# Moving four epilogue steps between two groups of a fused gated-attention and SoLU kernel: copies out of PSUM removed, finish(0), finish(1) and the next load of alpha moved ahead in the order

## The chip, the cores and the metric

The kernel runs on one core of a Trainium2 chip. The metric is the device time of one execution in microseconds (us), as the median of the runs; the profile shows one such execution. The engines of a core run side by side and wait for one another by semaphores: TensorE (PE; PEld is its loading of weights), VectorE (DVE), ScalarE (ACT), GpSimd (POOL) and SyncE (SP), which issues DMAs.

## The reference

Inputs q, k, v, alpha have the shape (4, 8, 768, 48): batch B, heads H, tokens S, head size D. For each batch and head a state is carried over the tokens:

```
state = alpha[t, :, None] * state + outer(k[t], v[t])
y[t]  = q[t] @ state
```

The y of all heads are laid side by side, 384 values per token (DM), and the 3072 tokens go through one block:

```
h    = x @ w_in                       # 384 -> 1024 (DFF)
solu = h * softmax(h)
ln   = (solu - mean) / sqrt(var + 1e-6) * g_ln
out  = ln @ w_out                     # 1024 -> 384
```

All arrays are float32 in the kernel; the weights come as float64 and are converted on the chip.

## The kernel before, in words

**Groups and chunks.** The tokens are cut into G = 6 groups of 128 positions; a group holds those positions of all 4 batches, so 512 tokens, or four *chunks* of 128 tokens each. Chunk n belongs to group n // 4 and batch n % 4. Attention is done chunk-wise for a group (scores within the 128 positions, plus a carried state); the block is done group by group.

**The steps of attention for a group g.** alpha_T(g) transposes alpha on VectorE into aT (L205); alpha_over(g) (L210) reads the loaded alpha twice on ScalarE for a check of its range; only after it may load(alpha, an, g + 1) (L138) fill the same buffer. scan_back(g, i) (L224) makes products of alpha from the end into hT, scan_on(g, i) (L229) products from the start into aT; both run on VectorE in three parts, and scan_on(g, 2) also has ScalarE copy fend. keys and queries are multiplied by these products into kT, qv and qe; apart() (L245) splits qe on ScalarE. scores(g, half) (L275) writes four PSUM banks a0 to a3 from PE; masked(half) (L289) moves them on VectorE under the triangular mask into sT, and scores of the other half need these banks again. decay(g) (L256) scales the carried state on GpSimd. read_state (L330) and read_values (L343) make y in the banks a0 to a3 on PE; read_values ends with four copies of y by ScalarE into x (L351). next_state(g) (L353) updates the state.

**The steps of the block.** up_mm(g, f) (L385) is h = x @ w_in for one of eight slices f of DFF, into one of two PSUM buffers "h"; up_act (L395) makes e = exp(h) on ScalarE, u = h * e on VectorE and u squared on ScalarE. down(n, half) (L494) multiplies u of chunk n by w_out, four *steps* (values of f) per half, into a PSUM tile "o", of which there are two buffers (ps_o, L73): o of chunk 2 needs the buffer of chunk 0 to be free, o of chunk 3 that of chunk 1. w_out has one column of ones more (DM + 1), so that the sum of u comes with the product. finish(n) (L511) reads that sum on VectorE (L523 to L528), for group 0 adds mean_sb times the sum (L533), takes the power -1/2 on GpSimd (L537, r), scales on ScalarE (L539, o_sb) and stores through SP (L540). mean(half) (L625) makes mean_sb out of w_out on PE, with ScalarE copying each half out of an "h" buffer. in_range(i) (L579) checks a piece of the float64 weights with two reads by ScalarE; bits(i) (L589) converts it on VectorE; scaled(i) (L613) multiplies by the gain on ScalarE.

**What sets the order.** The program is written under a manual schedule: every engine runs its instructions in the order of the program text, and each waits at the head of its queue until what it needs is there. The change lies in a stretch written out by hand, L757 to L827, between the loop over the slices of group 0 (L726) and the planned loop for groups 1 to 5 (L894). It ends group 0 (its down and finish), does attention for group 1, and prepares chunk 2 of attention ("group 2": alpha, scans, keys). The first PE work behind it is up_mm(1, 0) (L908).

In the kernel before, moved(n) (L505) copies o of chunk n, with its sum, from PSUM to SBUF on ScalarE as soon as down(n) is complete; finish(n) then works on the copy, so o of chunks 2 and 3 can begin while finish(0) and finish(1) are still to come:

```
down(2, 0); down(2, 1); scores(1, 0); masked(0)
finish(0); finish(1); alpha_over(1); load(alpha, an, 2)
down(3, 0); scores(1, 1); masked(1); finish(2); alpha_T(2)
```

Seven of the eight steps of down(3) come before read_values(1) on PE: down(3, 0) and three steps of down(3, 1), two and one of them between the parts of read_state. The last step of down(3, 1) and finish(3) come behind read_values(1).

Of the kernel before, what the change touches and what calls it, by code (L numbers as in the profile page):

```python
# [9 lines left out]
FP = mybir.dt.float32  # L10
# [6 lines left out]
P = 128  # L17
# [15 lines left out]
def fast_path(ctx, tc, q, k, v, alpha, moe_w_in, moe_w_out, moe_g_ln, out):  # L33
# [12 lines left out]
    nc = tc.nc  # L46
    B, H, S, D = q.shape
    NTOK, DM = out.shape
# [8 lines left out]
    HF = FC // 2  # L57
# [4 lines left out]
    def pool(name, bufs, **kw):  # L62
        return ctx.enter_context(tc.tile_pool(name=name, bufs=bufs, **kw))
# [4 lines left out]
    work = pool("work", 2)  # L68
# [65 lines left out]
    st = [dict() for _ in range(N)]  # L134
# [3 lines left out]
    def load(src, dst, g):  # L138
        t = slice(g * P, (g + 1) * P)
        for b in range(B):  # L140
            nc.sync.dma_start(
                out=dst[32 * b : 32 * b + 32].rearrange("t h u d -> t h (u d)"),
                in_=src[b, :, t, :].rearrange("h (t u) d -> t h (u d)", u=TQ),
            )
# [100 lines left out]
    def apart():  # L245
        for i in range(2):
            nc.scalar.mul(
                out=qv[:, H : 2 * H].rearrange("p (j i) t -> p j i t", i=2)[:, :, i], in_=qe, mul=parity[:, i : i + 1]
            )
# [6 lines left out]
    def decay(g):  # L256

        if g == 0:
            return
        for i in range(2):  # L260
            for rows, d in ((0, h4[:, i:H:2, 1:2]), (H, h4[:, H:NB, 1:2])):
                s = state[:, rows + i : rows + H : 2, all_of[i]]
                nc.gpsimd.tensor_tensor(out=s, in0=s, in1=d.to_broadcast([P, NP, D]), op=ALU.mult)  # L263
            nc.gpsimd.tensor_scalar(
                out=ends_state[:, :, i], in0=state[:, H + i : 2 * H : 2, last_of[i]], scalar1=parity[:, i : i + 1],
                scalar2=None, op0=ALU.mult,
            )

    def quarter(b):
        return slice(32 * b, 32 * b + 32)  # L270
# [18 lines left out]
    def masked(half, batches=range(B)):  # L289
        a = masks[half]  # L290
        for b in batches:
            nc.vector.tensor_tensor(  # L292
                out=sT[:, b, half * NP : half * NP + NP], in0=a[b], in1=mask[:, None, :].to_broadcast([P, NP, P]),
                op=ALU.mult,
            )

    def keys_back(g, t=None):
        t = t or banks("tp", [NP, P], 3)
        for j in range(NB):
            nc.tensor.transpose(out=t[j // NP][:, j % NP], in_=kT[:, j], identity=ident)  # L300
        for i in range(3):
            nc.scalar.copy(out=kg[:, NP * i : NP * i + NP], in_=t[i])
# [18 lines left out]
    def read_begin():  # L321
        reading["y"] = {}
        reading["begun"] = set()
# [54 lines left out]
    def u_of(g, f):  # L378
        return slots[((0, 5, 4), (1, 2, 3))[g % 2][f // 3]][:, T4 * (f % 3) : T4 * (f % 3) + T4]
# [114 lines left out]
    def down(n, half, part=slice(0, HF)):  # L494
        g, b = divmod(n, B)
        d = st[n]
        if half == 0 and part.start == 0:
            d["o"] = ps_o.tile([P, 512], FP, tag="o", name="o")
        for f in range(half * HF + part.start, half * HF + part.stop):
            nc.tensor.matmul(  # L500
                d["o"][:, 0 : DM + 1], lhsT=u_of(g, f)[:, b * P : b * P + P], rhs=w_out[:, f], start=(f == 0),
                stop=(f == FC - 1), skip_group_check=True,
            )

    def moved(n):  # L505

        o = work.tile([P, DM + 1], FP, name="o_mean")
        nc.scalar.copy(out=o, in_=st[n]["o"][:, 0 : DM + 1])
        st[n].update(o=o, moved=True)

    def finish(n):  # L511
        g, b = divmod(n, B)
        d = st[n]
        s, o = sums[:, n], d["o"][:, 0:DM]
        t0 = b * S + g * P
        if g == G - 1:
            o_sb = work.tile([P, DM], FP, name="o_sb")
            r = gr[g]["r"][:, b : b + 1]
            nc.scalar.activation(out=o_sb, in_=o, func=AF.Copy, scale=r)
            nc.scalar.dma_start(out=out[t0 : t0 + P, :], in_=o_sb)  # L520
            d.clear()
            return
        nc.vector.tensor_copy(out=s[:, 0:1], in_=d["o"][:, DM : DM + 1])  # L523
        t = small.tile([P, 1], FP, name="t")
        nc.vector.scalar_tensor_tensor(
            out=t, in0=s[:, 0:1], scalar=-1.0 / DFF, in1=s[:, 0:1], op0=ALU.mult, op1=ALU.mult
        )
        nc.vector.tensor_tensor(out=s[:, 3:4], in0=t, in1=gr[g]["s"][:, b : b + 1], op=ALU.add)  # L528
        if g == 0:

            if not d.get("moved"):
                o = work.tile([P, DM + 1], FP, name="o_mean")[:, 0:DM]
            nc.vector.scalar_tensor_tensor(  # L533
                out=o, in0=mean_sb, scalar=s[:, 0:1], in1=d["o"][:, 0:DM], op0=ALU.mult, op1=ALU.add
            )
        r = small.tile([P, 1], FP, name="r")
        nc.gpsimd.tensor_tensor(out=r, in0=s[:, 3:4], in1=mhalf, op=ALU.pow)  # L537
        o_sb = work.tile([P, DM], FP, name="o_sb")
        nc.scalar.activation(out=o_sb, in_=o, func=AF.Copy, scale=r)  # L539
        nc.sync.dma_start(out=out[t0 : t0 + P, :], in_=o_sb)  # L540
        d.clear()
# [35 lines left out]
    made = {}  # L577

    def in_range(i):  # L579


        if not float64:
            return
        hi = raws[i][:, :, :, 1].bitcast(FP)
        sq = one.tile([P, F], FP, name="sq").rearrange("p (c f) -> p c f", c=hi.shape[1])
        nc.scalar.activation(out=sq, in_=hi, func=AF.Square, accum_out=far[:, i, 0:1])  # L586
        nc.scalar.activation(out=sq, in_=sq, func=AF.Exp, scale=-(2.0**24), accum_out=far[:, i, 1:2])
# [37 lines left out]
    def mean(half):  # L625


        m = ps_h.tile([P, 512], FP, tag="h", name="sums")[:, 0:DM]
        if half == 0:
            for f in range(FC):  # L630
                r = quarter(f % 4)
                nc.tensor.matmul(
                    m[r], lhsT=ones[:, 0:32], rhs=w_out[:, f, 0:DM], start=f < 4, stop=f >= FC - 4,
                    tile_position=(0, r.start), skip_group_check=True,
                )
            made["m"] = work.tile([P, DM + 1], FP, name="o_mean")[:, 0:DM]
            nc.scalar.mul(out=made["m"], in_=m, mul=-1.0 / (32 * DFF))
        else:
            nc.tensor.matmul(m, lhsT=ones, rhs=made["m"], start=True, stop=True)
            nc.scalar.copy(out=mean_sb, in_=m)  # L640
# [32 lines left out]
    def three(name, where):  # L673
        return [pool.tile([P, NP, P], FP, tag=tag, name=f"{name}{i}") for i, (pool, tag) in enumerate(where)]
# [14 lines left out]
    for i in range(3):  # L689
        part = slice(NP * i, NP * i + NP)  # L690
# [6 lines left out]
    for i in (2, 0, 1):  # L697
        if i == 1:
            scan_on(0, i)
        part = slice(NP * i, NP * i + NP)  # L700
        nc.vector.tensor_tensor(  # L701
            out=qe if i == 2 else qv[:, part], in0=t[i], in1=aT[:, part, 1:SW], op=ALU.mult
# [68 lines left out]
    for i in range(3):  # L771
        scan_back(1, i)
        part = slice(NP * i, NP * i + NP)
        nc.vector.tensor_tensor(out=kT[:, part], in0=tk[i], in1=hk[:, part], op=ALU.mult)

    down(0, 1, slice(0, 2))
    mean(0)
    down(0, 1, slice(2, HF))
    moved(0)
    mean(1)  # L780
    in_range(5)
    down(1, 1)
    moved(1)
    tq += three("tp_q2", [(ps_h, "h")])
    turned(qn, ends_q, tq, range(H, NB))
    load(q, qn, 2)
    in_range(6)
    keys_back(1, three("tp", [(ps_a, "a2"), (ps_a, "a3"), (ps_h, "h")]))
    scan_on(1, 2)
    nc.vector.tensor_tensor(out=qe, in0=tq[2], in1=aT[:, H:NB, 1:SW], op=ALU.mult)  # L790
    apart()
    decay(1)
    in_range(7)
    for i in range(2):
        scan_on(1, i)
        part = slice(NP * i, NP * i + NP)
        nc.vector.tensor_tensor(out=qv[:, part], in0=tq[i], in1=aT[:, part, 1:SW], op=ALU.mult)
    down(2, 0)
    down(2, 1)
    scores(1, 0)  # L800
    masked(0)
    finish(0)
    finish(1)
    alpha_over(1)
    load(alpha, an, 2)
    down(3, 0)
    scores(1, 1)
    masked(1)
    finish(2)
    alpha_T(2)  # L810
    read_begin()
    for batches, part in (((0, 1), slice(0, 2)), ((2, 3), slice(2, 3))):
        down(3, 1, part)
        for n in range(len(parts)):
            read_state(n, batches)
    alpha_over(2)
# [6 lines left out]
    scan_on(2, 2)  # L823
    scan_on(2, 0)
    read_values(1)
    down(3, 1, slice(3, HF))
    finish(3)  # L827


# [64 lines left out]
    for g in range(1, G + 1):  # L894
# [10 lines left out]
        for s in range(FC):  # L905
# [17 lines left out]
            if step:  # L923
                n, half = step
# [23 lines left out]
    def compare(out, x, bound, op):  # L948
# [6 lines left out]
        out=chunks[:, :, 2], in0=sums[:, :, 2], scalar=0.25, in1=sums[:, :, 3], op0=ALU.mult, op1=ALU.is_le  # L955
# [6 lines left out]
    else:  # L962
# [9 lines left out]
        out=bad, in0=all_ok[0:1, 0:1], scalar1=float(P * ends[-1]), scalar2=None, op0=ALU.is_lt  # L972
# [451 lines left out]
```

## Time and profile before

| what | value |
|---|---|
| median of 3 runs | 391.65 us (391.28 to 392.57) |
| profiled execution, its own time | 391.28 us |
| its span, first to last instruction | 389.5 us |
| mean granted TensorE clock | 0.985 |
| busy in the span | PE 369.6 (95%), DVE 244.3 (63%), ACT 148.3 (38%), POOL 127.5 (33%) |
| alpha_over(1) on ACT, start | 94.00 us |
| alpha for chunk 2: first issue by SP, transposed from | 97.38 us, 103.97 us |
| read_values(1) on PE | 99.63 to 105.66 us |
| up_mm(1, 0) on PE, start | 112.10 us |

The page gives busy time by engine, a strip of the span in 40 slices (a digit is the busy share in tenths; PEclk is the clock granted to TensorE, in tenths), the chain of work that ended last, and groups of instructions by line. The other views are the trace's own: the waits (which engine waited for which, how long), the chain in order of time, the timeline (instructions of a window in order of time), and windows (busy time of each engine, clock and DMA share in a stretch). Instructions are named by tile and line: "PE o L500" is a matmul into o at line 500, which is down.

### The profile page before, as it was taken

What the parts mean: (1) busy time and instruction counts of PE and PEld (TensorE: products, weight loads), DVE (VectorE), ACT (ScalarE), POOL (GpSimd) and SP (SyncE); (2) the same over time, 40 slices, a digit from 0 to 9 for tenths busy, and PEclk for the clock granted to TensorE, in tenths of its full rate; (3) what the DMA queues carried; (4) which work ended last, traced back from release to release, by engine and by line L of the source; (5) the groups of instructions that cost most, each with busy time, mean ns of one, the idle gap of its engine ahead of it and who ended that gap; (6) DMA issues with size and microseconds to landing.
All of it is one profiled execution on the core that took longest, in us unless ns stands there. A gap on an engine that the chain in (4) does not pass through costs nothing.

```text
span 389.5 us, 10523 instructions
## 1 busy us (share of the span) xinstructions
PE 369.6 (95%) x4659; PEld 222.4 (57%) x4659; DVE 244.3 (63%) x379; ACT 148.3 (38%) x265; POOL 127.5 (33%) x132
## 2 busy tenths in 40 slices
PE   8869999999749999999999999999999999999995
PEld 8766345566525457556656656566555575555552
DVE  0985878987398877594655793665894511444410
ACT  3637775474324516125252224153223231333111
POOL 5030000042041994246423346422544620333210
PEclk9989999999969999999999999999999999999999
DMA  9981999301467300674000863000600000000011
GB/s 186 257 221 55 235 264 183 83 0 44 104 143 122 82 3 4 94 173 101 22 2 24 129 141 97 22 4 22 97 6 22 22 24 2 21 20 20 22 43 48
DMA packets 65510, 30.78 MB, mean 79 GB/s; under 512 B 47016, under 2 KB 63664, under 8 KB 65456
## 3 DMA queue, kind: packets, MB, share of 16 engines
q1 hardware_dynamic: 64432, 29.10, 34.5%
q10 hardware_dynamic: 1024, 0.92, 0.7%
q8 instruction: 38, 0.62, 0.7%
q14 instruction: 16, 0.13, 0.1%
HBM read 25.30 MB, written 4.72 MB: 77 GB/s over the span
## 4 chain that ended last, share of the span: by engine, by line
PE 67%; DVE 14%; ACT 7%; DMA 4%; SPq 4%; issue 3%; POOL 0%; ACTq 0%
PE o L500 28%; PE h L389 23%; PE y L315 9%; PE a L281 4%; DMA room<-in_v_dram 3%; SPq L153 2%; DVE room L404 2%; DVE aT L222 2%; DVE hT L222 2%; DMA an<-in_alpha_dram 1%; ACT sq L586 1%; DVE sT L292 1%; DVE aT L197 1%; PE kv L364 1%; PE tp L300 1%
## 5 line engine op out<-in xcount | busy, mean ns | idle before, releaser
L389 PE MATMUL h<-x,w_in 128*128 128x512 f32 x288 | 133.9, 604 | 6.1 <-ACT x L351 5.6
L500 PE MATMUL o<-w_out,room 128*128 128x385 f32 x384 | 133.8, 491 | 0.0
L500 PEld LDWEIGHTS o<-w_out,room 128*128 128x128 f32 x384 | 71.2, 190 | 55.8 <-issue 13.9
L389 PEld LDWEIGHTS h<-x,w_in 128*128 128x128 f32 x288 | 53.5, 192 | 66.0 <-issue 49.3
L404 DVE TENSOR_TENSOR room<-h,e 128x512 f32<-128x512 f32 x40 | 27.6, 690 | 82.4 <-ACT e L403 82.3
L403 ACT ACTIVATE e<-h 128x512 f32<-128x512 f32 x40 | 23.9, 597 | 107.7 <-PE h L389 107.7
L420 POOL TENSOR_TENSOR p<-p,e 128x512 f32<-128x512 f32 x30 | 41.8, 1395 | 16.0 <-ACT e L403 15.9
L537 POOL TENSOR_TENSOR r<-sums,mhalf 128x1 f32<-128x1 f32 x20 | 14.9, 745 | 79.6 <-DVE sums L528 79.5
L405 ACT ACTIVATE u<-room 128x512 f32<-128x512 f32 x40 | 25.2, 630 | 35.8 <-DVE room L404 35.8
L292 DVE TENSOR_TENSOR sT<-a,mask 128x512 f32<-128x512 f32 x42 | 26.1, 681 | 8.0 <-PE a L281 7.9
L243 POOL TENSOR_TENSOR kT<-kT,hT 128x1024 f32<-128x1024 f32 (+1 forms) x8 | 14.2, 1792 | 49.6 <-DVE kT L197 49.6
L315 PE MATMUL y<-sT,vn 128*32 128x128 f32 x768 | 25.1, 286 | 5.4 <-DVE sT L292 2.9
L263 POOL TENSOR_TENSOR state<-state,hT 128x192 f32<-128x192 f32 x20 | 11.2, 580 | 55.1 <-DVE hT L222 55.1
L222 DVE TENSOR_TENSOR_SCAN hT<-aT,unit 128x516 f32<-128x516 f32 x18 | 23.1, 1336 | 8.0 <-ACT aT L683 7.9
L222 DVE TENSOR_TENSOR_SCAN aT<-aT,seed 128x516 f32<-128x516 f32 x18 | 27.3, 1547 | 0.2
L420 DVE TENSOR_TENSOR p<-p,u 128x512 f32<-128x512 f32 x30 | 23.0, 768 | 6.5 <-ACT u L405 6.5
L315 PEld LDWEIGHTS y<-sT,vn 128*32 128x32 f32 x768 | 22.4, 115 | 7.7 <-issue 4.1
L281 PEld LDWEIGHTS a<-qv,kT 32*128 32x128 f32 x704 | 21.9, 186 | 8.0 <-issue 2.4
L281 PE MATMUL a<-qv,kT 32*128 32x128 f32 x704 | 24.7, 278 | 1.2 <-DVE qv L701 0.5
L214 ACT ACTIVATE sq<-an,mone 128x1536 uint8<-128x1536 f32 x12 | 18.9, 1573 | 6.4 <-DMA an<-in_alpha_dram 6.2
L315 PE MATMUL y<-qv,state 32*32 32x128 f32 x960 | 16.8, 277 | 0.0
L539 ACT ACTIVATE o_sb<-o,r 128x384 f32<-128x384 f32 x16 | 9.3, 581 | 18.7 <-POOL r L537 18.7
(146 smaller groups left out, 372.2 us busy)
## 6 DMA issues: line engine op xcount, KB each, us to landing
an<-in_alpha_dram SPq DMA_DIRECT2D x20, 192.0 KB, 4.2
vn<-in_v_dram SPq DMA_DIRECT2D x10, 384.0 KB, 5.2
out_dram<-o_sb SPq DMA_DIRECT2D x20, 192.0 KB, 1.9
room<-in_moe_w_in_dram SPq DMA_DIRECT2D x6, 512.0 KB, 6.5
room<-in_moe_w_out_dram SPq DMA_DIRECT2D x8, 384.0 KB, 3.9
kn<-in_k_dram SPq DMA_DIRECT2D x16, 192.0 KB, 4.3
qn<-in_q_dram SPq DMA_DIRECT2D x16, 192.0 KB, 3.6
kn<-in_k_dram SPq DMA_DIRECT2D x4, 384.0 KB, 5.7
```

The source lines that it names most:

```text
L214: nc.scalar.activation(out=sq, in_=x, func=AF.Relu, scale=sign, bias=mone, accum_out=over[:, g, i : i + 1])
L222: nc.vector.tensor_tensor_scan(out=o, data0=a, data1=s, initial=1.0, op0=ALU.mult, op1=ALU.add)
L281: nc.tensor.matmul(a[b][:, i], lhsT=kT[quarter(b), kb], rhs=qv[quarter(b), qb], start=kb == h, stop=kb != h, tile_position=(32 * b, 0), sk ...
L292: nc.vector.tensor_tensor(out=sT[:, b, half * NP : half * NP + NP], in0=a[b], in1=mask[:, None, :].to_broadcast([P, NP, P]), op=ALU.mult,)
L315: nc.tensor.matmul(y_bank(b)[quarter(r), a], lhsT=lhsT, rhs=rhs, start=(b, r) not in begun, stop=stop, tile_position=(row, 32 * r), skip_g ...
L389: nc.tensor.matmul(h, lhsT=w_in[:, a, f * P : (f + 1) * P], rhs=d["x"][:, a].rearrange("p b t -> p (b t)"), start=(a == 0), stop=(a == KC ...
L403: nc.scalar.activation(out=e, in_=h, func=AF.Exp)
L404: nc.vector.tensor_tensor(out=u, in0=h, in1=e, op=ALU.mult)
L405: nc.scalar.activation(out=u2, in_=u, func=AF.Square)
L420: eng.tensor_tensor(out=p, in0=d[0][i] if f == 1 else p, in1=d[f][i], op=ALU.add)
L500: nc.tensor.matmul(d["o"][:, 0 : DM + 1], lhsT=u_of(g, f)[:, b * P : b * P + P], rhs=w_out[:, f], start=(f == 0), stop=(f == FC - 1), skip ...
L537: nc.gpsimd.tensor_tensor(out=r, in0=s[:, 3:4], in1=mhalf, op=ALU.pow)
```

## The change

The function moved() and its two calls go; finish(n) of group 0 reads o in PSUM and writes a new tile. The tile o_mean loses its extra column. In the stretch by hand, mean(0) comes ahead of all of down(0, 1); in_range(6) comes ahead of down(1, 1); finish(0) comes behind apart() and ahead of decay(1); down(2, 1) comes behind scores(1, 0); finish(1), alpha_over(1) and load(alpha, an, 2) come ahead of masked(0); down(3, 0) is done in two halves between the parts of read_state, and all of down(3, 1) comes behind read_values(1). Nothing is added; the number of matmuls stays the same.

```
-    def moved(n):
-        o = work.tile([P, DM + 1], FP, name="o_mean")
-        nc.scalar.copy(out=o, in_=st[n]["o"][:, 0 : DM + 1])
-        st[n].update(o=o, moved=True)
...
-            if not d.get("moved"):
-                o = work.tile([P, DM + 1], FP, name="o_mean")[:, 0:DM]
+            o = work.tile([P, DM], FP, name="o_mean")
...
-    down(0, 1, slice(0, 2))
     mean(0)
-    down(0, 1, slice(2, HF))
-    moved(0)
+    down(0, 1)
     mean(1)
     in_range(5)
+    in_range(6)
     down(1, 1)
-    moved(1)
     tq += three("tp_q2", [(ps_h, "h")])
     turned(qn, ends_q, tq, range(H, NB))
     load(q, qn, 2)
-    in_range(6)
     keys_back(1, three("tp", [(ps_a, "a2"), (ps_a, "a3"), (ps_h, "h")]))
     scan_on(1, 2)
     nc.vector.tensor_tensor(out=qe, in0=tq[2], in1=aT[:, H:NB, 1:SW], op=ALU.mult)
     apart()
+    finish(0)
     decay(1)
     in_range(7)
...
     down(2, 0)
-    down(2, 1)
     scores(1, 0)
-    masked(0)
-    finish(0)
     finish(1)
     alpha_over(1)
     load(alpha, an, 2)
-    down(3, 0)
+    masked(0)
+    down(2, 1)
     scores(1, 1)
     masked(1)
     finish(2)
     alpha_T(2)
     read_begin()
-    for batches, part in (((0, 1), slice(0, 2)), ((2, 3), slice(2, 3))):
-        down(3, 1, part)
+    for batches, part in (((0, 1), slice(0, HF // 2)), ((2, 3), slice(HF // 2, HF))):
+        down(3, 0, part)
         for n in range(len(parts)):
             read_state(n, batches)
...
     read_values(1)
-    down(3, 1, slice(3, HF))
+    down(3, 1)
     finish(3)
```

## The prediction

> **What bounds the kernel now.** The page first. TensorE (PE) is busy 95% of the span, so time can only come from its few holes. The busy line shows one real hole, in slices 10 and 11 counted from 0 (97 to 117 us), and in the second of them the granted clock is low too:
>
> ```profile
> PE   8869999999749999999999999999999999999995
> ...
> PEclk9989999999969999999999999999999999999999
> ```
>
> Second the waits: what ended PE's idle time from 60 to 125 us. Columns: total us, times, longest.
>
> ```profile
> PE h L389 <- ACT x L351: 5.6, 1, 5.6
> PE y L315 <- issue: 2.0, 1, 2.0
> PE tp L300 <- DVE kT L774: 0.6, 1, 0.6
> ```
>
> The 5.6 us are up(1,0), the first projection of group 1, waiting for ScalarE's copies of y. Third, the chain that ended last, in order of time (start, us, what), says why those copies are late:
>
> ```profile
> 81.38 5.19 PE o L500 x16
> 86.57 1.99 PE a L281 x55
> ...
> 88.59 2.48 DVE sT L292 x4
> ...
> 92.58 0.87 POOL r L537
> ...
> 94.00 1.66 ACT sq L214 x2
> ...
> 98.76 5.19 DMA an<-in_alpha_dram
> ...
> 103.97 2.12 DVE aT L197
> ...
> 118.16 0.56 POOL r L537
> ...
> 118.74 0.61 ACT o_sb L539
> ...
> 119.36 0.49 ACT e L403
> ```
>
> Read it upwards: e(1,0), the first exponential, stands in ScalarE's queue behind finish(3), that in VectorE's queue behind the scans of chunk 2, those behind the load of alpha for chunk 2, that behind alpha_over(1) on ScalarE, that behind finish(1), that behind masked(0), and masked(0) behind scores(1,0) and eight down steps on PE. The copies of y stand behind the same scans, through the fend copy of scan_on(2,2). So this stretch is set by the moment at which alpha_over(1) starts: 94.00 us.
>
> **The change, part by part.** I go by the timeline's starts; PE, VectorE (DVE), ScalarE (ACT), GpSimd (POOL).
>
> 1. *moved(0), moved(1) go.* Two ACT copies of 0.48 us (74.92, 78.16), and in_range(6), which stood behind the second, starts at once behind in_range(5). I cost this at nothing: ACT's next copies (kg, 80.45) wait for transposes of kT, and DVE's chain reaches the last kT at 80.67 either way. Without that cover it would be a gain of at most 0.96.
>
> 2. *mean(0) ahead of down(0,1).* PE is free at 70.40, but mean(0) needs the PSUM bank that DVE's transpose of cols frees at 71.40; it ran 71.89 to 73.32 and will run about 71.5 to 72.9. PE stands 1.1 us, and the work to the end of keys_back moves from 81.38 to about 81.6. Nothing again, since PE then waits anyway (3).
>
> 3. *finish(0) ahead of decay(1) and two scans.* DVE: its four instructions took 90.99 to 91.97, so 0.98; they now start after qe (82.89) and end near 83.85, and the last product qv ends at 87.60 instead of 86.62. PE: down(2,0) takes the PSUM buffer that moved(0) used to free at 75.4; now it waits for finish(0), 81.6 to 83.85, a new idle of 2.2. It ends at 86.45 (2.6 for four steps: sixteen instructions took 5.19), and scores(1,0) waits until 87.60 for the bank that the last qv reads: 1.1 more, and 1.03 later than before (86.57). POOL: r(0) at about 83.4 to 84.3 (0.9, as at 91.61) stands ahead of decay(1), whose six instructions took 4.75 without their waits; it ends at 88.95, not 84.28. PE's read_state, which needs it, comes at 96. ACT: in_range(7) stands behind o_sb(0) and ends at about 86.9, before anyone needs ACT. SP: one more store stands ahead of alpha's load, issued (0.4) near 85, when SP's queue is empty (nothing from 73.1 to 93.1 in the profile).
>
> 4. *finish(1), alpha_over(1) and alpha's load ahead of masked(0).* This is the gain. finish(1) no longer waits for scores and masks: DVE 87.60 to 88.58. Its r(1) on POOL stands behind decay(1): 88.95 + 0.55 (the two later r's) = 89.5; o_sb(1) 89.6; alpha_over(1) at 90.1, against 94.00: **3.9 earlier**. Bounds: with POOL free r(1) would start at 88.1 and alpha_over at 89.3 (4.7 earlier); with decay(1) at its whole 6.18 (78.10 to 84.28, waits counted) and r at 0.9 it starts near 91.9 (2.1 earlier). The load then goes out at 93.5 instead of 97.38, and alpha lands at 100.1 instead of 103.97. DVE is free for it: masked(1) and finish(2) end near 98.0 (5). Four loads and one store move earlier with their order kept.
>
> 5. *What is late next: PE's own chain.* From 87.60 with measured lengths: scores(1,0) 2.05, down(2,1) 2.79, scores(1,1) 1.99 (masked(0), 89.6 to 92.05, is ready in time) end at 94.4; masked(1) 94.5 to 97.0. Two steps of down(3,0) 1.5, read_state 1.78, two more steps 1.4 (73.32 to 74.72), read_state 2.05: 101.2 (before: 99.62, although three steps fewer stand ahead of it). read_values took 5.97 with its 2.04 us stall, 3.93 without: it ends at 107.2 or 105.2. Then all four steps of down(3,1), 2.75, where one stood before: they fill what was idle. up(1,0) starts at 109.95 or, without the stall, when the copies are done: scans end at 110.28 - 3.9 = 106.4, the copies (110.43 to 112.05) at 108.2. It started at 112.10, and slowly: 4.38 against 2.79 at full clock.
>
> 6. *Where both meet.* up(1,2) started at 120.62, on DVE's release of h. DVE and ACT bring that to 120.62 - 3.9 = 116.75. PE, with the stall, gets there at 109.95 + 2.79 + 1.47 (kv) + 2.73 = 116.95. The later one decides: 3.7 earlier. From there PE is busy to the end in an unchanged order (134 to 389 us: 250 of 255), so the shift is kept.
>
> Sum: the profiled execution took 391.28 (389.5 in the span, 1.8 around it), so 387.6. The median of the runs, 391.65, lies 0.37 above it; the forecast for a median is **387.9**.
>
> **Two costs that the trace bounds only loosely.** The stall: PE stops for 2.04 us inside read_values for nothing the profile shows, while the load of alpha fills the DMA engines:
>
> ```profile
> 100.00:102.00 2.00, 1.58 (x59) 1.31 (x48) 0.00 (x0) 0.00 (x0) 0.00 (x0) 1.00 1.04 220
> 102.00:104.00 2.00, 0.38 (x16) 0.39 (x20) 0.03 (x1) 0.00 (x0) 0.00 (x0) 1.00 0.25 77
> ```
>
> (Columns: window, length, busy us and instructions of PE, PEld, DVE, ACT, POOL, then clock, DMA share, GB/s.) The page's instruction queue moved 38 packets for 0.62 MB; PE's 9318 instructions over 38 are some 245 to a packet. From 92.4 to 107 us PE will issue some 424 short matmuls with their loads, 848 instructions, so 3 to 4 packets, some of them under a load of alpha (93.5 to 100.1, and the next from about 103.5). Between no stall and four, I take one of 2.04 as seen.
> The Trainium skill ("Runtime: NRT & Kernel Launch", Instruction fetch mechanics) holds that instructions come in blocks of 256 and that crossing one is mostly hidden; by it the stall would cost nothing and the shift would be the 3.9 of part 4.
>
> The clock: idle of 2.86 us (22.25 to 25.10) is followed by 0.62 and 0.52 of the full clock from 26 to 30, and 120 matmuls of y then took 5.15, against 3.74 at the rate of the 128 later ones (3.99): 1.4 lost. The 2.04 us stall left the clock at 1.00. My new idles, 2.2 and 1.1 with 2.6 us of matmuls between, lie nearer the stall: I take no loss, with 1.4 to 1.6 (4.38 - 2.79) as the other end.
> The Trainium skill ("TensorE: Matmul & The Clock Gate", Part 1: The HAM clock gate) has the clock fall after an idle window of about 3.4 us; by it neither idle would cost anything, though the 2.86 us row shows that less was enough here.
>
> **The rivals.** (a) *The clock falls* at 83.9 us, or decay(1) is as slow as its bound: PE's chain loses 1.6, or alpha's chain keeps 2.1 of 3.9; the shift is about 2.1: 389.5. For it: the 2.86 us row. Against: a stall of 2.04 did nothing.
> (b) *A second stall.* Each adds 2.04 to PE's chain, which has 0.0 to spare: 3.7 - 2.04 = 1.6, so 390.0.
> (c) *Slower:* PE's chain becomes the bound and stalls three times more in read_state, read_values and kv, because both loads of alpha now lie beside dense matmuls, where the second lay beside an idle PE: 3.7 - 6.1 = 2.4 slower, 394.1. It decides once the added stalls exceed 3.7 us. For it: 3 to 4 packets fall in that stretch; against: one stall in the whole profile before.
> (d) *Nothing moves:* the gain of 3.7 is given back by two more stalls, or alpha's load takes its time under PE's fetches: within 1.2 us of 391.65.
>
> **Numbers.** Forecast 0.58, (a) 0.13, (b) 0.11, (d) 0.09, (c) 0.09. Faster by over 0.3% (1.2 us, about what a measurement of this kernel can tell from no change): 0.58 + 0.13 + 0.11 = 0.82; within it 0.09; slower 0.09. The range leaves out (c) and (d), 0.18: from the early bound of part 4 (391.65 - 4.7, so 386.9) to (b) with a little more, 390.4.
>
> **What would show it.** Right: alpha_over(1) starts near 90.1, alpha lands near 100.1, PE waits for finish(0) near 82 to 84 and hardly for x before up(1,0), which runs at full clock from about 110. Wrong: POOL's r(1) later than 91; the clock below 1.0 between 84 and 92; more than one wait of PE for "issue"; or up(1,2) near 120 although alpha landed at 100, in which case a later bound hid the shift.

## The result, and the profile after

| | before | after |
|---|---|---|
| median | 391.46 us (4 runs, 391.11 to 392.57) | 385.86 us (4 runs, 384.77 to 386.53) |
| profiled execution, its span | 391.28, 389.5 | 386.53, 384.7 |
| TensorE busy in the span | 369.6 | 367.6 |
| mean granted clock | 0.985 | 0.995 |

The ratio is 0.9849, 95% interval [0.9816, 0.9883]: 5.6 us less by the medians. The forecast was 387.9 in a range from 386.9 to 390.4, so the sign held and the size was too small by 2 us; the time lies below the range.

The strip of the page has no hole any more in slices 10 and 11, and the clock is full there; a smaller one has come in slices 7 and 8, where PE now waits for mean(0)'s bank and for finish(0):

```profile
PE   8769999879999999999999999999999999999995
...
PEclk9989999999999999999999999999999999999999
```

The waits of PE in after, 60 to 125 us (total us, times, longest). The 5.6 us for x are gone, and the stall for "issue" has shrunk from 2.0 to 0.2. Four waits are new, and all are for VectorE: o_mean is finish(0), cols is the bank of mean(0), room is the release of h for up(1,2), and qv is the bank of scores(1,0):

```profile
PE o L500 <- DVE o_mean L526: 2.4, 1, 2.4
PE sums L625 <- DVE cols L460: 1.0, 1, 1.0
PE h L389 <- DVE room L404: 0.8, 1, 0.8
PE a L281 <- DVE qv L787: 0.4, 1, 0.4
PE y L315 <- issue: 0.2, 1, 0.2
```

The chain of after in order of time (start, us, what). masked(0) is no longer a link between the scores and alpha's load; from the load on, the same steps follow as before, some 4 to 5 us earlier:

```profile
88.10 2.06 PE a L281 x62
90.16 2.79 PE o L500 x8
92.95 0.56 PE a L281 x13
93.53 0.34 SPq L141
...
94.91 4.36 DMA an<-in_alpha_dram
99.29 2.21 DVE aT L197
...
113.78 0.55 POOL r L530
114.35 0.61 ACT o_sb L532
114.97 0.50 ACT e L403
115.49 0.70 DVE room L404
```

The view puts scores(1,1) ahead of the load, whose PE work ends at 93.51 us; by the program the load waits for alpha_over(1), and that ends on ScalarE at 93.50. alpha_over(1) itself starts behind finish(1)'s o_sb, which waited for r on GpSimd and no longer for scores and masks. ScalarE's timeline of after:

```profile
89.63 0.61 ACT L532 ACTIVATE o_sb<-o_mean,r 128x384 f32<-128x384 f32 x1 [2.56 <-POOL r L530]
90.15 1.56 ACT L214 ACTIVATE sq<-an,mone 128x1536 uint8<-128x1536 f32 x1
```

**One zero for all profiles.** The opening takes a different time in each execution: the last product kT of group 1, behind which nearly all of the changed stretch lies, starts at 79.98 us in the profile of before and at 80.50 in a second one of the same kernel (e9), at 80.44 in after and at 81.30 in a second one (e0); in the twelve experiments it lies between 78.43 and 81.42 (e7). I therefore count from its start. Most of the differences that are left come from the stretch itself (us; the end is known to 0.1; "stall" is PE's wait for "issue" at y L315 inside read_values; "load" is SP's first issue of alpha for chunk 2, "aT" its transposition):

```
                          alpha_over  load    aT     up(1,0)  e(1,0)   end   stall
before                      14.02    17.40   23.99    32.12   39.28  309.52  2.04
e9   before, again          14.02    17.40   24.53    32.63   39.80  310.60  2.04
after                        9.71    13.09   18.85    27.99   34.43  304.26  0.22
e0   after, again            9.70    13.08   18.93    29.27   34.44  304.50  0.75
e1   before, alpha alone     6.18     9.57   16.94    25.35   32.44  302.60  0.94
e2   after, alpha back      13.72    17.10   23.17    31.29   38.46  308.67  1.65
e3   before, down(3)        14.02    17.39   24.99    33.14   40.32  310.17  1.67
e4   after, moved() back    10.13    13.51   20.71    30.77   36.14  306.81  0.27
e5   before, copies ahead   14.03    17.41   24.57    29.55   37.56  309.79  2.04
e6   before, both            6.18     9.57   16.94    25.31   30.05  301.11  0.94
e7   before, no loads       14.03      -    16.95    25.32   32.47  302.58  0.94
e8   e4 with PE filled      10.13    13.51   19.05    29.13   34.55  304.43  0.52
e10  before, store late     14.01    17.39   23.51    33.24   39.83  311.47  1.49
e11  after, PE late          9.71    13.09   18.80    30.32   34.30  305.77  none
```

By this count after ends 5.26 us earlier than before (309.52 - 304.26), and e(1,0) stands 4.85 earlier. Two executions of one kernel differ here too: by the second profiles of both (e9, e0) the end is 6.10 earlier. The 5.6 of the medians is not told from 5.26: the interval of the ratio is 2.6 us wide. Steps 1 and 2 of the change lie ahead of the zero; the four starts of it above show no gain or loss that could be told from their scatter.

### The profile page after: what moved, and what is told of

Same layout as the page of the kernel before. It is cut to its first block, busy times and chain, and to the rows that moved or that the text cites. A ratio compares the mean times of both kernels' runs of the same rounds, so it can differ in the third digit from the quotient of the medians.

```text
span 384.7 us, 10520 instructions
## 1 busy us (share of the span) xinstructions
PE 367.6 (96%) x4659; PEld 221.5 (58%) x4659; DVE 244.3 (64%) x379; ACT 147.4 (38%) x263; POOL 126.6 (33%) x132
## 4 chain that ended last, share of the span: by engine, by line
PE 70%; DVE 14%; SPq 5%; DMA 5%; ACT 3%; issue 2%; POOL 0%; DVEq 0%; ACTq 0%
PE o L500 28%; PE h L389 25%; PE y L315 9%; PE a L281 4%; SPq L153 3%; DVE aT L222 3%; DMA room<-in_v_dram 3%; DMA an<-in_alpha_dram 2%; DVE hT L222 2%; PE kv L364 1%; DVE room L404 1%; SPq L562 1%; DVE aT L197 1%; PE tp L300 1%; SPq L141 1%
## 5 line engine op out<-in xcount | busy, mean ns | idle before, releaser
L389 PE MATMUL h<-x,w_in 128*128 128x512 f32 x288 | 132.3, 598 | 1.3 <-DVE room L404 1.3
L405 ACT ACTIVATE u<-room 128x512 f32<-128x512 f32 x40 | 25.2, 630 | 35.5 <-DVE room L404 35.5
L315 PE MATMUL y<-sT,vn 128*32 128x128 f32 x768 | 24.8, 284 | 3.9 <-ACT vn L193 3.6
L315 PEld LDWEIGHTS y<-sT,vn 128*32 128x32 f32 x768 | 21.9, 114 | 6.4 <-ACT vn L193 4.3
L315 PE MATMUL y<-qv,state 32*32 32x128 f32 x960 | 16.6, 277 | 0.0
L315 PEld LDWEIGHTS y<-qv,state 32*32 32x32 f32 x960 | 12.1, 103 | 6.9 <-issue 4.9
## 6 DMA issues: line engine op xcount, KB each, us to landing
vn<-in_v_dram SPq DMA_DIRECT2D x10, 384.0 KB, 5.2
room<-in_moe_w_out_dram SPq DMA_DIRECT2D x8, 384.0 KB, 4.0
kn<-in_k_dram SPq DMA_DIRECT2D x4, 384.0 KB, 5.7
```

Of the source, the lines that this page charges most:

```text
L315: nc.tensor.matmul(y_bank(b)[quarter(r), a], lhsT=lhsT, rhs=rhs, start=(b, r) not in begun, stop=stop, tile_position=(row, 32 * r), skip_g ...
L389: nc.tensor.matmul(h, lhsT=w_in[:, a, f * P : (f + 1) * P], rhs=d["x"][:, a].rearrange("p b t -> p (b t)"), start=(a == 0), stop=(a == KC ...
L405: nc.scalar.activation(out=u2, in_=u, func=AF.Square)
```

## The experiments

Each run stands beside executions of before taken with it, whose median went from 390.62 to 392.11 us. So the runs are compared by their ratios to before, and a difference in us is the ratio's share of 391.65.

**e0, after once more.**

> The changed kernel itself, for a narrower interval. The one profile of it is 4.75 us shorter than the one of before, the medians differ by 5.6; up to the first kT of group 1 both kernels run the same code, yet the profile of the changed one is 0.46 us late there. Theory A (alpha's chain) and theory B (TensorE's own order) both give the same again: 385.9, 5.2 to 5.7 under the kernel before. The last kT of group 1 starts between 79.5 and 80.5 us.

Measured: 386.13 us, ratio 0.9858 [0.9833, 0.9884]. The result holds. Its profile shows what after's doesn't: the clock fell. PE's timeline of e0 (start, us, instructions, idle before and its releaser), with down(2,0) at 4.52 us where after has 2.83 for the same eight matmuls behind the same idle:

```profile
85.31 4.52 PE L500 MATMUL o<-w_out,room 128*128 128x385 f32 x8 [2.39 <-DVE o_mean L526]
89.76 2.07 PE L281 MATMUL a<-qv,kT 32*128 32x128 f32 x64
```

and the windows of e0 (the third number from the end is the granted clock):

```profile
84.00:86.00 2.00, 0.69 (x2) 0.49 (x3) 1.93 (x6) 1.78 (x4) 1.28 (x2) 1.00 0.00 0
86.00:88.00 2.00, 2.00 (x5) 1.05 (x4) 1.97 (x3) 1.88 (x5) 1.90 (x3) 0.53 0.26 98
88.00:90.00 2.00, 2.00 (x12) 0.79 (x14) 1.90 (x6) 0.00 (x0) 1.90 (x5) 0.62 0.00 0
```

So rival (a) of the prediction did happen here, and it cost PE 0.8 us (the scores 8.46 behind the zero, against 7.66 in after). With a stall of 0.75 instead of 0.22, up(1,0) came 1.28 later than in after. PE had 0.82 to spare there, its wait for room in after; e(1,0) came at the same 34.44, and the end 0.2 later.

**e1, alpha alone.** Before, with one move: alpha_over(1) and the load go up past finish(0), finish(1) and the scores.

```
     in_range(7)
+    alpha_over(1)
+    load(alpha, an, 2)
     for i in range(2):
...
     finish(1)
-    alpha_over(1)
-    load(alpha, an, 2)
     down(3, 0)
```

> The kernel before with one thing moved: alpha_over(1) and the load of alpha for chunk 2 stand behind in_range(7) on ScalarE, ahead of finish(0), finish(1) and masked(0). TensorE's order is that of the kernel before. Theory A (the start of alpha_over(1) sets the stretch): alpha_over(1) at 86.1 instead of 94.0, alpha there at 95.3 to 96.1, VectorE free for it at 97.0, so its chain is 7.0 earlier; up(1,0) starts near 106 behind the copies of y; 384.5, that is 7 us faster than before and 1.4 faster than the change. Theory B (the gain came from three down steps fewer ahead of read_values): TensorE's order is unchanged, so 391.5, at best 1.6 less for an up(1,0) at full clock.

Measured: 384.09 us, ratio 0.9805 [0.9773, 0.9837], 7.6 us less. The start of alpha's load alone brings all of the gain, and more than the whole change: e0, taken beside it, has a median of 386.13, and the end is 1.66 earlier than after's, though the intervals of the ratios overlap a little. The chain of e1 shows where this ends: alpha has landed before VectorE is ready for it, and the scores, masked(1) (sT) and finish(2) are what comes last ahead of its transposition:

```profile
91.94 2.03 PE a L281 x64
93.98 2.46 DVE sT L292 x4
...
97.34 2.12 DVE aT L197
```

The load is issued 7.83 us earlier than in before, and aT follows by 7.05.

**e2, the rest without alpha.** After, with masked(0) put back ahead of finish(1) and the load.

```
     scores(1, 0)
+    masked(0)
     finish(1)
     alpha_over(1)
     load(alpha, an, 2)
-    masked(0)
     down(2, 1)
```

> The changed kernel with finish(1), alpha_over(1) and the load of alpha put back behind masked(0). Theory A: alpha_over(1) starts near 94.0 again, alpha is there near 103.4, and the gain is lost: 390.0 to 391.0; what is left is up(1,0) at full clock, up to 1.6. Theory B: the order of TensorE is the changed one, so 386 to 387.

Measured: 390.18 us, ratio 0.9975 [0.9953, 0.9997]. By putting back one line all but 1 us (0.1 to 1.8) of the gain is gone. That is what all other parts of the change together are worth here; by the table 0.8 of it is that alpha is there earlier (23.17 against 23.99): the load is issued 0.30 earlier and takes 0.52 less.

**e3, down(3) alone.** Before, with down(3,0) in two halves between the parts of read_state and all of down(3,1) behind read_values(1).

```
-    down(3, 0)
     scores(1, 1)
...
-    for batches, part in (((0, 1), slice(0, 2)), ((2, 3), slice(2, 3))):
-        down(3, 1, part)
+    for batches, part in (((0, 1), slice(0, 2)), ((2, 3), slice(2, HF))):
+        down(3, 0, part)
...
-    down(3, 1, slice(3, HF))
+    down(3, 1)
```

> The kernel before with only the steps of down(3) redistributed as in the change: four ahead of read_values(1), in two halves, and four behind it. Theory A: read_values ends about 2 us earlier, but the copies of y and e(1,0) still wait for the scans of chunk 2: 391.5 within 0.8. Theory B: three steps of 0.65 us leave the path, 389.5.

Measured: 391.42 us, ratio 0.9998 [0.9977, 1.0018]: nothing that can be seen. PE's waits in e3 say why: the steps of down(3) that now stand behind read_values shorten a wait, and the wait's end stays with ScalarE's copies of y:

```profile
PE h L389 <- ACT x L351: 3.4, 1, 3.4
PE y L315 <- issue: 1.7, 1, 1.7
```

**e4, finish(0) without its wait on PE.** After, with moved() and its calls back, so that down(2,0) need not wait for finish(0). All else keeps its place in after: finish(0) still stands ahead of decay(1) and of the scores, and mean(0) and in_range(6) are not put back.

```
...
     down(0, 1)
+    moved(0)
     mean(1)
...
     down(1, 1)
+    moved(1)
```

> The changed kernel with the copies moved(0) and moved(1) put back, its order otherwise kept: o of chunk 2 no longer waits for finish(0), so TensorE's idle of 2.4 us ahead of down(2,0) goes. Theory A (VectorE's chain through alpha decides): no change against the changed kernel, 385.5 to 386.5. Rival: TensorE's new idle is paid in full, and the time falls by up to 2.4 to 383.6.

Measured: 387.52 us, ratio 0.9890 [0.9863, 0.9916], 1.3 to 1.6 us more than after and e0 by the ratios, whose intervals overlap, and 2.3 to 2.6 more at the end by the table, although a wait of 2.4 us is gone. The wait has moved: down(2,0) runs at once, and then PE stands idle ahead of the scores in two pieces with a burst of 0.48 us between them. PE's timeline of e4:

```profile
80.55 2.76 PE L500 MATMUL o<-w_out,room 128*128 128x385 f32 x8
84.89 0.48 PE L281 MATMUL a<-qv,kT 32*128 32x128 f32 x2 [1.57 <-DVE qv L796]
86.76 3.79 PE L281 MATMUL a<-qv,kT 32*128 32x128 f32 x62 [1.39 <-DVE sums L523]
90.48 3.92 PE L500 MATMUL o<-w_out,room 128*128 128x385 f32 x8
```

The scores took 2.06 us in after and down(2,1) 2.86. The clock of e4 in these windows:

```profile
86.00:88.00 2.00, 1.24 (x22) 1.25 (x26) 1.84 (x5) 0.00 (x0) 1.90 (x4) 0.50 0.00 0
88.00:90.00 2.00, 2.00 (x43) 2.00 (x42) 0.00 (x0) 1.29 (x2) 0.67 (x2) 0.50 0.03 8
90.00:92.00 2.00, 2.00 (x13) 1.16 (x10) 1.80 (x3) 1.97 (x3) 0.00 (x0) 0.50 0.28 98
```

Here the slow PE reaches alpha's chain: masked(1) and finish(2) end at 99.8 us, 20.7 behind the zero, and hold up the transposition of alpha.

**e8, the same with PE kept at work.** e4 with 28 matmul instructions, whose output nobody uses, between down(2,0) and the scores.

```
     down(2, 0)
+    warm(14, ps_h, "h")
     scores(1, 0)
```

> The kernel is e4 (after with moved() and the old places of mean(0), down(0,1), in_range(6) put back, so that finish(0) stands behind the scores and PE no longer waits for it) with 28 matmul instructions added between down(2,0) and scores(1,0), whose output nobody uses. In e4 PE stood idle there from 83.2 to 86.8 us but for a short burst, and the clock was 0.50 from 86 to 92 us; scores(1,0) took 3.79 us where after has 2.06, down(2,1) 3.92 where after has 2.86. Theory clock: the idle before the scores lowered the clock, so work that fills it brings the scores back to about 2.1 us, down(2,1) to about 2.9, the clock to 1.00 in 86 to 92 us, and the time to the 385.5 to 386.5 us of after, although work was added. Theory copies: e4's loss of 1.4 us against after comes from the copies that ScalarE makes again and from finish(0) standing ahead of finish(1); then the added work gains nothing, the time stays at 387.5 or more, and the scores still take over 3 us or their speed does not matter.

The kernel differs from e4 by the added matmuls alone; what the expectation says in brackets of mean(0), down(0,1), in_range(6) and finish(0) is not so, as said under e4.

Measured: 386.33 us, ratio 0.9877 [0.9849, 0.9905]. The trace is that of the clock theory: a clock of 1.00 in every window from 82 to 94 us, the scores in 2.45 and down(2,1) in 2.86 us, and the end 2.38 earlier than e4's, level with after:

```profile
84.83 3.29 PE L445 MATMUL warm<-ones 128*128 128x128 f32 x28
88.05 2.45 PE L281 MATMUL a<-qv,kT 32*128 32x128 f32 x64
90.42 2.86 PE L500 MATMUL o<-w_out,room 128*128 128x385 f32 x8
```

The times are weaker evidence: the ratios of e8 and e4 differ by 0.0013, 0.5 us, and their intervals overlap. That the clock falls behind the idle, and stays up with work in its place, is shown by one trace each; what it is worth in the time is not settled.

**e5, the copies of y ahead of the scans.** Before, with the last two scans of chunk 2 behind read_values(1) and finish(3).

```
     load(k, kn, 3)
-    scan_on(2, 2)
-    scan_on(2, 0)
     read_values(1)
     down(3, 1, slice(3, HF))
     finish(3)
+    scan_on(2, 2)
+    scan_on(2, 0)
```

> The kernel before with scan_on(2,2) and scan_on(2,0) put behind read_values(1), the last step of down(3,1) and finish(3), so that ScalarE's copies of y, its o_sb(3) and e(1,0) no longer stand behind the scans of chunk 2. alpha_over(1) stays at 94.0. Reading 1 (the longest wait of TensorE, 5.6 us for the copies, is the cost): up(1,0) starts near 109 instead of 112.1 and the kernel is 3 us faster, 388.3. Reading 2 (VectorE's queue is the bound, and the product u of slice 0 stands behind the same scans either way): that product starts at 118.6 instead of 119.87, so 1.3 us, 390.0.

Measured: 390.31 us, ratio 0.9943 [0.9923, 0.9963], 2.2 us less (1.4 to 3.0), about midway between the two readings. In the trace PE's wait for x shrinks from 5.6 to 0.9 us, but PE then waits 3.3 for VectorE's release of h. The prediction named two reasons for what comes late behind read_values, the copies and finish(3). The copies now come early; e(1,0), at 37.56, still stands behind finish(3), whose two small steps on VectorE took 1.31 and 1.10 us beside GpSimd's product kT (0.16 each in before); and the product u stands behind the two scans, 0.64 earlier than in before, not the 1.27 of reading 2. The end is 0.3 later than in before and 0.8 earlier than in e9, so the one profile doesn't show the gain of the times; how large it is stays open.

**e6, e1 and e5 together.**

> The kernel before with both moves: alpha_over(1) and the load of alpha behind in_range(7), and the two scans of chunk 2 behind finish(3). Theory A with reading 2: the 1.3 us add to the 7 of the first move, since TensorE still waited 1.5 us for VectorE there: 382.8, faster than both kernels. If TensorE's own chain takes over, nothing is added: 384.1.

Measured: 383.47 us, ratio 0.9777 [0.9748, 0.9806]. This is the lowest ratio here, below those of both kernels. From e1 it is not told by the times, whose intervals overlap; by the table the end is 1.5 us earlier than e1's, near the 1.3 of the expectation. Its edit is that of e1 and that of e5, and none of the change's other steps. In its waits PE has hardly anything left for VectorE (1.5 us in e1):

```profile
PE y L315 <- issue: 0.9, 1, 0.9
...
PE h L389 <- DVE room L404: 0.2, 1, 0.2
```

**e7, no load at all.**

```
     alpha_over(1)
-    load(alpha, an, 2)
     down(3, 0)
...
     alpha_over(2)
-    load(alpha, an, 3)
```

> The kernel before without the loads of alpha for chunks 2 and 3 (groups 2 and 3 go on with the alpha of group 1), to see the stall of TensorE in read_values(1) with no load in flight. So far it sat at the 63rd matmul of read_values in the kernel before and at the 68th or 69th in the kernels with six matmuls fewer ahead, that is at one running number of instructions, and lasted 0.2 to 2.0 us. If a load under way makes it: under 0.3 us. If it is there whatever the DMA engines do: 0.8 to 2. VectorE starts alpha_T(2) at 97 instead of 104, so about 7 us faster by theory A: 384.5.

Measured in one profile, 385.78 us; the output is not that of the reference, since the loads are left out. The span is 384.0 us and the last kT starts at 81.42, so the end, 302.6 behind the zero, is 6.9 earlier than in before, as theory A has it (7). The stall is still there, 0.94 us, at the same matmul as in before (the 64th of read_values waits). PE's timeline of e7:

```profile
104.01 2.04 PE L315 MATMUL y<-sT,vn 128*32 128x128 f32 x65 [0.94 <-issue]
```

So the load isn't its cause, but in this order it is longer with one: 2.04 us in both profiles of before. Over all fourteen profiles: where the load of alpha for chunk 2 ran up to that point (DMA share 0.72 to 1.05 in the 2 us ahead of the stall), 2.04, 2.04, 2.04, 1.67, 1.65 and 1.49 us (before, e9, e5, e3, e2, e10; e5 has one of 0.51 before it); where it had landed, or was not loaded (share 0 to 0.08), 0.22 to 0.94 (after, e0, e1, e4, e6, e7), and in e8 0.60 and 0.52 in two pieces. These two sets don't overlap. But e11 had no stall at all, with the next load at a share of 0.94 to 1.09 from 105 to 108 us, all through read_values: a load alone doesn't make PE stop either.

**e9 and e10, the landing of alpha.** e9 is before, unchanged. In e10 finish(2) stands behind scan_back(2), so that its store isn't issued while alpha is in flight.

```
     masked(1)
-    finish(2)
     alpha_T(2)
...
         scan_back(2, i)
+    finish(2)
     keys_T(2)
```

> The kernel before, unchanged, profiled once more. If the stall inside read_values and the landing of alpha are fixed by the program, they are again 2.0 us and 6.6 us; if they vary from execution to execution, the stall lies anywhere from 0.9 to 2.1 us and the landing anywhere from 5.8 to 7.6 us, and differences of that size between two profiles say nothing of the change. The start of the last product kT, 79.98 us in the first profile, should lie between 78.4 and 81.3 us.

> The kernel before with finish(2) put behind scan_back(2), so that its store is issued only when alpha has landed. Theory store: in before the store of chunk 2, which is issued while the load of alpha is in flight, makes the load land late; then first issue to transposed goes from 6.59 to about 5.8 us, as in after. Theory chance: the landing varies with the execution or with where the weights' code is fetched; then it is 6.5 us or more, or anywhere from 5.8 to 7.6. The time itself may rise by up to 1 us, since finish(2) now takes VectorE's time on the path of the scans, and is not what the run is for.

Measured: from the first issue to the transposition 7.13 us in e9 (before: 6.59), with the stall at 2.04 again; 6.12 in e10. Their times are single ones, 392.9 us for e9 and 394.49 for e10; the end of e10 is 0.9 to 2.0 later than in e9 and before, with up to 1 expected. e9's last kT starts at 80.50 us, inside the range expected. Where VectorE waited for the data and no store lay in between, it was 5.76 (after) and 5.54 (e8). The store of 192 KB is thus a likely part of the longer landing, 0.5 to 1.0 us of it, but 0.5 also lies between two profiles of one kernel, and e2 (6.07), e5 (7.16) and e3 (7.60), all with the store, don't fit a simple sum. How much is the store's stays open.

**e11, PE late on purpose.** After, with 18 matmul instructions, whose output nobody uses, ahead of read_values(1), so that PE comes out of it about as late as the stall of before would have made it.

```
     scan_on(2, 0)
+    warm(9, ps_h, "h")
     read_values(1)
```

> The kernel after, with 18 matmul instructions more between the last read_state and read_values(1), whose output nobody uses: about 2.0 us of PE work (28 of the same took 3.12 us), so that PE comes out of read_values as late as the stall of 2.04 us seen in before would have made it. Theory A: in after PE's chain has some slack against VectorE's and ScalarE's, and the stall of 2.04 us that the prediction kept was a real price. In after PE waited 0.82 us for VectorE's product (room) ahead of up(1,2); so up(1,2) comes 2.0 - 0.8 = 1.2 us later, counted from the last product kT, and the time is about 1.2 us above after, 387.0 to 387.4 beside a median of before of 391.5 (ratio 0.988 to 0.990): most of the way back to the forecast of 387.9. Theory B: the chain through alpha, scans and ScalarE sets the end alone and PE catches up; then the time stays at after's 385.9 to 386.2 (ratio 0.985 to 0.986), and PE's wait ahead of up(1,2) is gone without a later start. Theory C: the added work also delays the copies of y on ScalarE and so e(1,0); then the loss is 2 us or more (387.9 or more).

Measured: 387.05 us, ratio 0.9871 [0.9835, 0.9906], an interval that holds theories A and B. The trace tells them apart. PE's timeline of e11:

```profile
85.04 4.52 PE L500 MATMUL o<-w_out,room 128*128 128x385 f32 x8 [2.37 <-DVE o_mean L526]
...
102.82 2.27 PE L445 MATMUL warm<-ones 128*128 128x128 f32 x18
105.02 3.70 PE L315 MATMUL y<-sT,vn 128*32 128x128 f32 x128
...
111.35 2.74 PE L389 MATMUL h<-x,w_in 128*128 128x512 f32 x6
...
115.50 5.42 PE L389 MATMUL h<-x,w_in 128*128 128x512 f32 x12
```

up(1,0) starts 2.33 us later than in after (30.32 against 27.99 from the zero). PE had 0.82 to spare, its wait for room in after; 2.33 - 0.82 = 1.51 is left, and the end is 1.5 later (305.77 against 304.26). e(1,0) has not moved (34.30): theory C falls, and B too, since the wait for room is gone and the end has moved. The 2.33 are the added 2.2, and 0.75 for the clock, which fell here too (0.50 and 0.68 from 86 to 90 us), less the stalls and gaps that went. The 0.75 are not the experiment's, and this execution was the slowest of six: they took 384.84 to 388.63 us, in step with their mean granted clock, 0.999 to 0.986. Without the 0.75 the same sum leaves 0.8 us for the added work. So that lateness of PE reaches the end is shown in the trace; the 1.2 of theory A is not measured to better than 0.5 to 1.5.

## Why the prediction was too small

By its own steps, counted from the zero (the prediction's times less 79.98):

1. *moved() goes, mean(0) goes ahead: nothing.* Nothing could be seen; PE waited 0.98 us for cols, with 1.1 forecast.
2. *finish(0) ahead (part 3).* As forecast on VectorE. PE's idle was 2.39 and 0.41 us, with 2.2 and 1.1 forecast. The clock, of which the prediction took no loss, held in after and fell in e0 and e11: a loss of 0.8 us on PE in some executions. The row of 2.86 us, given there as speaking for rival (a), was the better guide. The one against it, "a stall of 2.04 did nothing", held in the profile of before alone: behind the same stall of 2.04 the clock fell in e9 (0.76 and 0.50 from 104 to 108 us) and in e5 (0.60 and 0.55), and the 65 matmuls that took 2.04 in before took 3.24 and 3.71. PE's timeline of e9:

```profile
104.37 3.24 PE L315 MATMUL y<-sT,vn 128*32 128x128 f32 x65 [2.04 <-issue]
```

3. *alpha_over(1) (part 4).* 3.9 earlier forecast, 4.31 measured: r(0) on POOL took 0.54 us and not 0.9, and r(1) started 8.59 behind the zero, with 8.97 forecast. A size off by 0.4, inside the given bounds.
4. *The landing (part 4).* Taken as 6.59 as in before; it was 5.76, so another 0.83. The steps from there to e(1,0) took 0.29 longer (15.58 against 15.29). 4.31 + 0.83 - 0.29 makes the 4.85 at e(1,0). Of the shorter landing the prediction had no term, and how much of it is the store's and how much chance stays open (e9, e10).
5. *PE's own chain (part 5).* The sum without the stall was right: read_values was to end 25.2 behind the zero, and down(3,1) started at 25.29; up(1,0) was to start at 28.0 if PE alone decided, and started at 27.99.
6. *Where both meet (part 6): this step failed.* "The later one decides: 3.7 earlier" rested on the term "Between no stall and four, I take one of 2.04 as seen". The stall measured 0.22 us. So PE didn't decide: it waited 0.82 for VectorE, and up(1,2) followed the chain of alpha: it starts 35.79 behind the zero, 4.85 earlier than in before, with 36.97 forecast. The last 0.4 of the 5.26 came behind it in small steps on PE, spread over the rest of the span.

By the forecast's own sums each of the two errors alone would have been nearly hidden. With 4.85 on the chain of alpha and the stall kept, PE would have decided, 3.7 earlier; with the stall gone and the chain of alpha as forecast, the gain would have been 3.9. Only both together give 5. e11 is the test of the first case: a later PE decides there. That it ends 3.75 us earlier than before, so near to 3.7, is luck, as the fallen clock made up 0.75 of PE's lateness.

The profile of before did hold a warning on the stall. In before it stood from 101.6 to 103.6 us, with alpha in flight, DMA share 1.04 and 0.25. The prediction's own times put alpha's landing at 100.1, read_values from 101.2 and the next load from about 103.5: the stall's place falls between two loads. The windows of after (the last three numbers are clock, DMA share, GB/s) show just that, with read_values from 101.48 to 105.7:

```profile
100.00:102.00 2.00, 2.00 (x124) 1.80 (x110) 2.00 (x2) 1.97 (x3) 0.00 (x0) 1.00 0.29 107
102.00:104.00 2.00, 1.78 (x64) 1.51 (x57) 2.00 (x3) 0.71 (x2) 0.00 (x0) 1.00 0.08 15
104.00:106.00 2.00, 2.00 (x61) 1.80 (x57) 2.00 (x3) 0.21 (x2) 0.00 (x0) 1.00 1.02 263
```

The prediction copied the stall as if it belonged to the program, without placing it in the new order. What length it would have there, the profile of before couldn't say: it was 0.22 us in after, 0.75 in e0 and 0.94 in e7. The page of the Trainium skill that it weighed ("Runtime: NRT & Kernel Launch", Instruction fetch mechanics: crossing a block is mostly hidden) came nearer with after's 0.22 us than the row of 2.04 did, though not with the 0.94 of e7.

The range failed for a second reason. Its low end came from one bound, POOL free in part 4 (4.7 earlier). A landing shorter than 6.59 and the scatter of the opening, which a single profile can't show and which is 3.0 us wide over all profiles, had no place in it.

The rivals: (a) came true in part, in e0 and e11, and cost little in e0 because PE had 0.82 us to spare; (b) and (c) asked for more stalls, and there were fewer; (d) is ruled out by the interval.

## What to carry to other kernels

When a step moves, move the waits that were measured near it too: ask for each stall of the old profile whether what lay beside it (a load in flight, an idle stretch ahead) is still beside it in the new order, and price both cases. Where two chains meet, a change in either one only counts up to the slack of the other: write both arrival times down with their own errors, and let the range hold the case in which both come early. And to start a load earlier, look first for the shortest move that does it: two lines moved ahead of two scans, the scores, a mask and two finishes (e1) gained more than the whole rearrangement.

## What the runs showed of the hardware

- The clock fell behind an idle of 2.37 and 2.39 us in two profiles (e11, e0: 0.50 to 0.68 for about 4 us) and did not behind the same idle in two others (after 2.39, e2 2.38: 1.00 from 80 to 90 us). Behind a stall of 2.04 us it held in before and fell in e9 and e5. In e4 two idles of 1.57 and 1.39 us with 0.48 us of matmuls between them gave 0.50 for 6 us. The clock gate's page of the Trainium skill ("TensorE: Matmul & The Clock Gate", Part 1: The HAM clock gate) has it fall after an idle window of about 3.4 us; here less was enough, and the same idle didn't always do it.
- PE stopped in a dense run of small matmuls with no wait that the profile shows, behind the 63rd to 69th in twelve profiles of fourteen: 0.22 to 0.94 us where no load ran in the 2 us ahead, 1.49 to 2.04 where one did. In e8, with 28 matmuls more ahead, it stopped behind the 41st and once before; in e11, with 18 more, not at all. That it is the fetch of instructions is an inference from the packets of the instruction queue, not shown.
- The same load of four times 192 KB took 6.59 and 7.13 us from issue to use in two profiles of one kernel.
